# Spreading the weight sums over half units, and splitting the store and the read-back of turned probabilities, in a sparse-attention and FFN kernel

## The chip, the cores and the metric

The kernel runs on one core of one Trainium2 chip. The metric is the device time of one execution in microseconds (us), as the median of several runs. The engines are named as in the profile: PE is TensorE (PEld its weight loads), DVE is VectorE, ACT is ScalarE, POOL is GpSimd, and SP is SyncE, which in this kernel only issues DMAs. Each engine works through its own instructions in the order of the program and stops at the first one whose inputs or buffers aren't ready.

## The reference

```python
def _attn_ref(q, k, v):            # (8, 8, 576, 64) each, float32
    scores = scale * np.matmul(q, k.transpose(0, 1, 3, 2))
    mask_local = (rel >= 0) & (rel < 32)                       # heads 0-3
    mask_strided = (rel >= 0) & (pos[None, :] % 32 == pos[:, None] % 32)   # heads 4-7
    scores = np.where(masks, scores, -1e9)
    attn = np.exp(scores - scores.max(-1))
    return np.matmul(attn / (attn.sum(-1) + 1e-09), v)

def _moe_ref(x, w_in, w_out):      # x (4608, 512), w_in (512, 2048), w_out (2048, 512)
    h = x @ w_in
    g = np.where(h >= 1, h, np.where(h <= -1, 0.0, (h + 1) ** 2 / 4))
    return g @ w_out
```

The attention's output, 8 batches of 576 tokens with 8 heads of 64, is the FFN's x: 4608 tokens of 512.

## The kernel before

**The FFN** takes most of the time. Each value is split into a rounded high part and a remainder, and a product is three matmuls (high by high, high by low, low by high). The tokens are done in two ways. The first 1536 are done in three chunks c = 0, 1, 2 of 512 tokens. A chunk has 16 units (c, f), one for each block of 128 of the 2048 hidden columns: `up` (L589) is 12 matmuls of 512 columns into one of two PSUM banks; `gate` (L611) is a chain ACT, ACT, DVE, ACT, DVE (L603, L606, L609, L622, L625) that makes the two parts `gh` and `gl`; `down` (L631) multiplies the gated blocks of two units, 24 matmuls at every other unit. The remaining 3072 tokens are done in three super-chunks s = 0, 1, 2 of 1024 tokens by a Strassen-Winograd scheme with 7 products in place of 8: `up_block` (L699) has 56 steps of 6 matmuls (L722), `down_block` (L788) 28 steps of 12 (L828). Each step needs a weight block that SP fetches from device memory into a ring of seven buffers `wr` (`fetch_w`, L660), one fetch behind each step, so that a fetch has seven steps to land.

**The weight sums.** Strassen-Winograd needs sums of weight blocks, made while the chunks c = 1 and c = 2 run. `combine(i, j, w32, st)` (L239) does one of the 16 sums that the schedule `COMBINE` (L913) lists: POOL adds the high and low parts back together into `w32` (L244, two operations of 512 elements in each partition), makes four sums of blocks in `st` (L252, four operations of 256); ACT rounds them (L254), DVE takes the remainder (L255), and SP stores `st` to device memory (`ks`, L256). The six POOL operations, the ACT, the DVE and the SP instruction are issued together, in the first half of a unit: at units (1, 0), (1, 1), (1, 2), (1, 4), (1, 5), (1, 6), (1, 8), (1, 9), (1, 10), and (2, 4), (2, 5), (2, 7), (2, 8), (2, 9), (2, 11), (2, 12). The room for `w32` and `st` is one buffer each (in chunk 1 a part of the tile for the first super-chunk's tokens that isn't yet needed, in chunk 2 the places of weights that are done with), so that a sum can be written only when the last one has been stored.

**The attention** of batch 0 lies before everything, batch 1 in chunk 0; batches 2 to 7 are laid out by hand among the FFN's steps. The place of a step is counted in quarters of a unit, g = 4 x (16 x (c - 1) + f) in the chunks, and one step of `up_block` is one g, one of `down_block` two. So chunk 1 is g 0 to 63, chunk 2 is 64 to 127, super-chunk 0 is 128 to 239, super-chunk 1 is 240 to 351. `START` (L896) has the g at which a batch begins, `LATER` (L897) what follows at which distance. A batch has four parts u = 0 to 3, and each part runs through named steps: `s` scores on PE (L343), `m` mask on DVE (L394), `x` maximum on DVE (L405), `a` subtract it on POOL (L409), `e` exponential on ACT (L416), `q` sum on DVE, `p` add the small constant on ACT, `r` reciprocal on DVE and the product on POOL (L433), `t` 32 x 32 transposes on DVE into two tiles (`turn`, L462), `j` the rest of the transposition by way of device memory (`spread`, L474), `v` the product with the values on PE (L500), and `h`, `l`, copies out of PSUM into the tokens' tiles (L554, L563).

`spread` stores the two turned tiles with eight DMAs that put each 32 x 32 block where it belongs (L484), and reads the whole back with one (L485), which must wait until the eight have landed. The turned tiles come from a pool `o_p` of three buffers (tag `ob`), which `down` also uses for a chunk's four output tiles `ob` (L643), and part 1 for its result `pT`; the other parts' `pT` has one buffer of its own.

**The tokens' sums and splits** for the first super-chunk (`x_sum`, `x_split`, by `X_FIRST`, L915) are at units (2, 9) to (2, 15), those for the next ones at steps of `down_block` (`X_NEXT`, L968).

Of the kernel before, what the change touches and what calls it, by code (L numbers as in the profile page):

```python
# [8 lines left out]
F32 = mybir.dt.float32  # L9
F32R = mybir.dt.float32r  # L10
# [15 lines left out]
def tile_sparse_attention_then_ffn(  # L26
# [79 lines left out]
    def slot(tag, shape, dtype, name):  # L106

        return big.tile(shape, dtype, tag=tag, bufs=1, name=name)
# [130 lines left out]
    def combine(i, j, w32, st):  # L239


        for f in range(2):
            parts = [wt[2 * j + f][:, i, :, x].bitcast(F32) for x in range(2)]
            nc.gpsimd.tensor_tensor(out=w32[:, 2 * f:2 * f + 2], in0=parts[0], in1=parts[1], op=ALU.add)  # L244

        def block(r, c):
            return w32[:, 2 * r + c if i == 0 else 2 * c + r]

        s_ = [st[:, n, HF:].bitcast(F32) for n in range(4)]
        for to, a, b, op in ((0, block(1, 0), block(1, 1), ALU.add), (1, s_[0], block(0, 0), ALU.subtract),  # L250
                             (2, block(0, 0), block(1, 0), ALU.subtract), (3, block(0, 1), s_[1], ALU.subtract)):
            nc.gpsimd.tensor_tensor(out=s_[to], in0=a, in1=b, op=op)  # L252
        hi, lo = st[:, :, :HF], st[:, :, HF:]
        nc.scalar.copy(hi.bitcast(F32R), lo.bitcast(F32))  # L254
        nc.vector.tensor_tensor(out=lo.bitcast(F32R), in0=lo.bitcast(F32), in1=hi.bitcast(F32), op=ALU.subtract)  # L255
        nc.sync.dma_start(kept[i][j][1].rearrange("p n x e -> p n (x e)"), st)  # L256
# [50 lines left out]
    def attention(b, kinds):  # L307

        probs, flipped, ahead, covered = {}, {}, {}, set()
# [164 lines left out]
        def spread(u):  # L474

            ts = probs.pop(u)
            n = sum(slots(u))
            pool, tag = (o_p, "ob") if u == 1 else (pt_p, "pT")
            pT = pool.tile([P, 4, n if u == 1 else 2 * SLOTS, ST], F32, tag=tag, name=f"pT_{b}_{u}")
            there = dram.tile([P, 4, n, ST], F32, tag=f"t{u}", name=f"there_{b}_{u}")  # L480
            for i in range(4):
                for h in range(2):
                    to = there[h * 64:(h + 1) * 64, i].rearrange("(k c) n q -> c k (n q)", c=ST)
                    nc.sync.dma_start(to, ts[h][i * ST:(i + 1) * ST, :, :n])  # L484
            nc.sync.dma_start(pT[:, :, :n], there)  # L485
            flipped[u] = pT
# [71 lines left out]
        def low(u):  # L558
            if u not in flipped:
                return  # L560
            for src, to in parts(u):
                if len(to) == 2:
# [4 lines left out]
                 "f": flip, "t": turn, "j": spread, "c": keep, "d": keep_v, "v": value, "V": values_1_3, "h": high, "l": low}  # L567
# [295 lines left out]
    with tc.manual_schedule():  # L863
# [19 lines left out]
        for k in range(2):  # L883
# [12 lines left out]
        START = {2: 0, 3: 33, 4: 69, 5: 112, 6: 150, 7: 240}  # L896
        LATER = {0: ("s0", "m0 x0 a0"), 3: ("", "e0"), 6: ("s1", "q0 p0 r0 m1 x1 a1"), 9: ("", "t0 j0 e1"),  # L897
# [15 lines left out]
        COMBINE = {(1, 4 * n // 3): (n >= NP, n % NP) for n in range(NP + 1)}  # L913
        COMBINE |= {(2, 3 + 4 * n // 3): (1, n) for n in range(1, NP)}
        X_FIRST = {9: (1,), 10: (2,), 13: (-7, -6, 7), 14: (-4, -5, 6), 15: (5,)}  # L915
        pend = []
        for c in range(CLASSIC):
            for f in range(NF):
# [24 lines left out]
                if c:  # L943
                    steps(g0, g0 + 2, 1)
                    ship(f, c - 1)
                    if (c, f) in COMBINE:
                        i, j = COMBINE[c, f]
                        if c == 1:
                            w32, st = (x_tile(0)[:, :, e0:e1] for e0, e1 in ((704, 960), (192, 704)))
                        else:  # L950
                            w32, st = (slot(X_AT[m], [P, 4, n], F32, f"{a}_{j}") for m, n, a in ((3, HF, "w32"), (4, CH, "st")))
                        combine(i, j, w32, st)
                    if c == 2:
                        x_steps(0, *X_FIRST.get(f, ()))
# [13 lines left out]
        X_NEXT = {8: (1,), 9: (2,), 10: (-7,), 11: (-6,), 12: (7,), 13: (-4,), 14: (-5,), 15: (6,), 18: (5,), 20: (3,), 27: (4,)}  # L968
# [76 lines left out]
```

## Time and profile before

| | us |
|---|---|
| time, median of 3 runs | 988.71 (985.37 to 990.67) |
| the profiled execution: time | 987.04 |
| the profiled execution: span of its instructions | 985.3 |
| PE busy | 857.5 (87%) |
| DVE busy | 555.8 (56%) |
| ACT busy | 495.7 (50%) |
| POOL busy | 236.7 (24%) |

Times in the views are counted from the first instruction of the profiled execution. A matmul's duration overlaps with the next one's, so that 12 matmuls of about 0.4 us each take less than 3 us together. A view of the waits says which engine stood still, in front of which line, for whose result, in us in total, how many times, and the longest. The chain of waits is followed back from the last instruction, at each step to what released it. In a row of the timeline the bracket behind an instruction has the idle time before it and what ended that. The granted clock is TensorE's, as a share of full speed.

### The profile page before, as it was taken

What the parts mean: (1) busy time and instruction counts of PE and PEld (TensorE: products, weight loads), DVE (VectorE), ACT (ScalarE), POOL (GpSimd) and SP (SyncE); (2) the same over time, 40 slices, a digit from 0 to 9 for tenths busy, and PEclk for the clock granted to TensorE, in tenths of its full rate; (3) what the DMA queues carried; (4) which work ended last, traced back from release to release, by engine and by line L of the source; (5) the groups of instructions that cost most, each with busy time, mean ns of one, the idle gap of its engine ahead of it and who ended that gap; (6) DMA issues with size and microseconds to landing.
All of it is one profiled execution on the core that took longest, in us unless ns stands there. A gap on an engine that the chain in (4) does not pass through costs nothing.

```text
span 985.3 us, 17928 instructions
## 1 busy us (share of the span) xinstructions
PE 857.5 (87%) x6965; PEld 679.3 (69%) x6965; DVE 555.8 (56%) x822; ACT 495.7 (50%) x852; POOL 236.7 (24%) x244
## 2 busy tenths in 40 slices
PE   8999967767698865868889798998889989999997
PEld 6788846645576654646667586776777867887886
DVE  6899715433344344355476477755546874455664
ACT  5888713323334334235665454455665454676442
POOL 5454245636011564220221100012100000001000
PEclk8999988969799997989999899999999999999999
DMA  9917316555466465447677675667566657666664
GB/s 360 376 36 256 113 55 227 197 175 194 127 217 202 141 219 197 149 154 262 213 246 242 216 226 169 216 211 229 165 197 182 210 185 225 192 194 180 214 192 160
DMA packets 102565, 195.12 MB, mean 198 GB/s; under 512 B 15184, under 2 KB 28240, under 8 KB 101584
## 3 DMA queue, kind: packets, MB, share of 16 engines
q1 hardware_dynamic: 102480, 193.97, 61.0%
q8 instruction: 55, 0.90, 0.4%
q14 instruction: 30, 0.25, 0.1%
HBM read 147.26 MB, written 46.66 MB: 197 GB/s over the span
## 4 chain that ended last, share of the span: by engine, by line
PE 44%; DVE 16%; DMA 12%; ACT 11%; POOL 9%; issue 5%; SPq 3%; ACTq 0%; DVEq 0%; POOLq 0%
PE y L722 9%; PE yo L828 8%; PE h L599 6%; PE o L640 6%; DMA wr<-ks 5%; PE z L722 4%; DVE hl L691 4%; PE xo L828 3%; ACT hl L690 3%; PE xp L500 2%; POOL xs L252 2%; PE x L722 2%; SPq L484 2%; POOL st L252 2%; DMA there<-t 2%
## 5 line engine op out<-in xcount | busy, mean ns | idle before, releaser
L722 PE MATMUL y<-x,wr 128*128 128x512 f32 x576 | 148.1, 404 | 20.2 <-DMA wr<-kq 7.3
L640 PE MATMUL o<-gh,w 128*128 128x512 f32 x384 | 134.9, 418 | 28.7 <-ACT gh L622 23.1
L599 PE MATMUL h<-xq,w 128*128 128x512 f32 x576 | 148.8, 410 | 3.7 <-DVE gl L625 2.8
L722 PEld LDWEIGHTS y<-x,wr 128*128 128x128 f32 x576 | 109.7, 194 | 49.6 <-DVE gb L609 6.2
L828 PE MATMUL yo<-hl,wr 128*128 128x512 f32 x576 | 136.9, 395 | 7.4 <-DVE hl L691 4.7
L599 PEld LDWEIGHTS h<-xq,w 128*128 128x128 f32 x576 | 111.8, 198 | 30.2 <-DVE gl L625 3.2
L828 PEld LDWEIGHTS yo<-hl,wr 128*128 128x128 f32 x576 | 108.6, 190 | 34.0 <-DVE hl L691 7.8
L640 PEld LDWEIGHTS o<-gh,w 128*128 128x128 f32 x384 | 76.7, 200 | 49.3 <-ACT gh L622 26.4
L409 POOL TENSOR_TENSOR pr<-pr,st 128x768 f32<-128x768 f32 (+3 forms) x31 | 37.6, 1213 | 238.4 <-DVE st L405 218.4
L722 PE MATMUL z<-x,wr 128*128 128x512 f32 x288 | 75.8, 400 | 8.3 <-DMA wr<-ks 8.2
L640 PE MATMUL o<-gl,w 128*128 128x512 f32 x192 | 79.7, 415 | 1.1 <-DVE gl L625 1.1
L828 PE MATMUL zo<-hl,wr 128*128 128x512 f32 x288 | 68.8, 394 | 5.4 <-DVE hl L691 4.1
L433 POOL TENSOR_TENSOR pr<-pr,st 128x648 f32<-128x648 f32 (+3 forms) x30 | 35.8, 1193 | 152.2 <-DVE st L432 151.3
L722 PEld LDWEIGHTS z<-x,wr 128*128 128x128 f32 x288 | 54.3, 190 | 21.3 <-DMA wr<-ks 4.0
L828 PEld LDWEIGHTS zo<-hl,wr 128*128 128x128 f32 x288 | 53.5, 188 | 20.2 <-DVE hl L691 6.7
L690 ACT CAST hl<-ga 128x1024 fp32r<-128x1024 f32 x36 | 37.9, 1052 | 51.2 <-DVE ga L781 20.5
L756 POOL TENSOR_TENSOR ga<-gb,ga 128x1024 f32<-128x1024 f32 x9 | 21.6, 2397 | 170.5 <-DVE ga L609 169.8
L606 ACT ACTIVATE tmp<-tmp 128x512 f32<-128x512 f32 x96 | 60.7, 632 | 1.7
L609 DVE SCALAR_TENSOR_TENSOR h<-h,u 128x512 f32<-128x512 f32 x47 | 32.7, 695 | 48.1 <-ACT u L606 47.8
L691 DVE TENSOR_TENSOR hl<-ga,hl 128x1024 fp32r<-128x1024 f32 x36 | 44.3, 1232 | 27.2 <-ACT hl L690 27.2
L343 PE MATMUL sc<-qk 64*32 64x64 f32 (+1 forms) x1856 | 35.6, 242 | 23.7 <-DVE xq L563 16.7
L500 PE MATMUL xp<-pT,v 64*64 64x32 f32 (+2 forms) x1760 | 35.2, 234 | 22.1 <-DMA pT<-there 11.4
(122 smaller groups left out, 1337.8 us busy)
## 6 DMA issues: line engine op xcount, KB each, us to landing
wr<-ks SPq DMA_DIRECT2D x192, 256.0 KB, 3.5
wr<-kq SPq DMA_DIRECT2D x144, 256.0 KB, 3.2
raw<-in_w SPq DMA_DIRECT2D x30, 512.0 KB, 9.6
kq<-w SPq DMA_DIRECT2D x48, 256.0 KB, 4.0
qk<-in_qk_s SPq DMA_DIRECT2D x16, 604.0 KB, 6.6
qk<-in_qk_l SPq DMA_DIRECT2D x16, 576.0 KB, 7.1
ks<-xs SPq DMA_DIRECT2D x9, 1024.0 KB, 5.3
v<-in_v_l SPq DMA_DIRECT2D x21, 384.0 KB, 5.6
```

Source lines behind the costliest of these rows:

```text
L252: nc.gpsimd.tensor_tensor(out=s_[to], in0=a, in1=b, op=op)
L343: nc.tensor.matmul(sc[j][i * Q:(i + 1) * Q, s, p], qk[:, 0, q0:q0 + Q], qk[:, 1, k0:k0 + W], start=u not in covered, stop=u not in covered)
L409: eng.tensor_tensor(out=pr, in0=pr, in1=st[:, 0].unsqueeze(2).broadcast_to(list(pr.shape)), op=ALU.add)
L433: eng.tensor_tensor(out=pr, in0=pr, in1=st[:, 2].unsqueeze(2).broadcast_to(list(pr.shape)), op=ALU.mult)
L500: nc.tensor.matmul(xp[p][j * D:(j + 1) * D, n], loaded[b, local, b0 + n][keys, j], qs, start=True, stop=True)
L599: nc.tensor.matmul(o_ps[c, f], wt[f][:, 0, h, x, e:e + P], xq[c][:, y, cc], start=first and n == 0, stop=last and n == len(todo) - 1)
L606: nc.scalar.activation(u, u, AF.Square)
L640: nc.tensor.matmul(o_ps[c][d], wt[f][:, 1, h, x, e:e + P], gs[y], start=f == 0 and n == 0, stop=f == NF - 1 and n == 2)
L690: nc.scalar.copy(t[:, 0], src)
L691: nc.vector.tensor_tensor(out=t[:, 1], in0=src, in1=t[:, 0].bitcast(F32), op=ALU.subtract)
L722: nc.tensor.matmul(to, w_[:, a, c * P:(c + 1) * P], xc[m][:, b, c], start=m in (1, 2, 5) and c + q == 0, stop=c == 1 and q == 2, skip_grou ...
L828: nc.tensor.matmul(to, w_[jj][:, a, d * P:(d + 1) * P], t[:, b, jj], start=m in (1, 2, 5) and k + jj + q == 0, stop=k == NP // 2 - 1 and j ...
```

## The change

**Sums.** `combine` is cut in three: `recall` (the two POOL adds of L244), `combine` (the four POOL operations of L252) and `ship_sums` (ACT, DVE and the store). A helper `sums(h)` is called twice in a unit, once in each half, h counting halves from the start of chunk 1. At half h it issues the `recall` of the sum due at h + 1, then the `combine` of the sum due at h, then the `ship_sums` of the one due at h - 1. The sums are due at every third half: h = 0, 3, ..., 24 in chunk 1 and 39, 42, ..., 57 in chunk 2. The first `recall` moves into the end of chunk 0.

**Turned probabilities.** `j` only stores, with two DMAs, one for each turned tile; a new step `J` (`gather`) allocates `pT` and reads it with four DMAs, one for each group of 32 partitions, which do the rearranging. `j` is now two quarters behind `t`, and `J` three behind `j` (`j` and the reading were in the same quarter as `t`).

**Batches.** `START` and some places of `LATER` move: `v2` and `t3` from 33 to 35, the last values from 42 to 45. `X_FIRST` and `X_NEXT` move by about a unit or a step.

```diff
+    def recall(i, j, w32):
+        for f in range(2):
+            hi, lo = (wt[2 * j + f][:, i, :, x].bitcast(F32) for x in range(2))
+            nc.gpsimd.tensor_tensor(out=w32[:, 2 * f:2 * f + 2], in0=hi, in1=lo, op=ALU.add)
+
     def combine(i, j, w32, st):
-        for f in range(2):
-            parts = [wt[2 * j + f][:, i, :, x].bitcast(F32) for x in range(2)]
-            nc.gpsimd.tensor_tensor(out=w32[:, 2 * f:2 * f + 2], in0=parts[0], in1=parts[1], op=ALU.add)
...
+    def ship_sums(i, j, st):
         hi, lo = st[:, :, :HF], st[:, :, HF:]
-        nc.scalar.copy(hi.bitcast(F32R), lo.bitcast(F32))
-        nc.vector.tensor_tensor(out=lo.bitcast(F32R), in0=lo.bitcast(F32), in1=hi.bitcast(F32), op=ALU.subtract)
+        nc.scalar.copy(hi.bitcast(F32R), lo)
+        nc.vector.tensor_tensor(out=lo.bitcast(F32R), in0=lo, in1=hi, op=ALU.subtract)
         nc.sync.dma_start(kept[i][j][1].rearrange("p n x e -> p n (x e)"), st)
...
             ts = probs.pop(u)
             n = sum(slots(u))
+            there[u] = to = dram.tile([P, 2, 2, n, ST], F32, tag=f"t{u}", name=f"there_{b}_{u}")
+            for h in range(2):
+                nc.sync.dma_start(to[:, h], ts[h][:, :, :n])
+
+        def gather(u):
...
-            there = dram.tile([P, 4, n, ST], F32, tag=f"t{u}", name=f"there_{b}_{u}")
-            for i in range(4):
-                for h in range(2):
-                    to = there[h * 64:(h + 1) * 64, i].rearrange("(k c) n q -> c k (n q)", c=ST)
-                    nc.sync.dma_start(to, ts[h][i * ST:(i + 1) * ST, :, :n])
-            nc.sync.dma_start(pT[:, :, :n], there)
+            src = there.pop(u).rearrange("(i c) h k n q -> h k c i (n q)", c=ST)
+            for h in range(2):
+                for k in range(2):
+                    at = h * 64 + k * ST
+                    nc.sync.dma_start(pT[at:at + ST, :, :n].rearrange("p i n q -> p i (n q)"), src[h, k])
...
-        START = {2: 0, 3: 33, 4: 69, 5: 112, 6: 150, 7: 240}
-        LATER = {0: ("s0", "m0 x0 a0"), 3: ("", "e0"), 6: ("s1", "q0 p0 r0 m1 x1 a1"), 9: ("", "t0 j0 e1"),
-                 12: ("s2", "q1 p1 r1 m2 x2 a2"), 15: ("", "t1 j1 e2"), 18: ("v0", "h0 l0"),
-                 21: ("s3", "m3 x3 a3 q2 p2 r2"), 24: ("", "t2 j2 e3"), 28: ("", "q3 p3 r3"),
-                 33: ("v2", "h2 l2 t3 j3"), 42: ("V1", "h1 l1 h3 l3")}
+        START = {2: 0, 3: 37, 4: 72, 5: 118, 6: 155, 7: 240}
+        LATER = {0: ("s0", "m0 x0 a0"), 3: ("", "e0"), 6: ("s1", "q0 p0 r0 m1 x1 a1"), 9: ("", "t0 e1"), 11: ("", "j0"),
+                 12: ("s2", "q1 p1 r1 m2 x2 a2"), 14: ("", "J0"), 15: ("", "t1 e2"), 17: ("", "j1"),
+                 18: ("v0", "h0 l0"), 20: ("", "J1"), 21: ("s3", "m3 x3 a3 q2 p2 r2"), 24: ("", "t2 e3"), 26: ("", "j2"),
+                 28: ("", "q3 p3 r3"), 29: ("", "J2"), 35: ("v2", "h2 l2 t3"), 37: ("", "j3"), 40: ("", "J3"),
+                 45: ("V1", "h1 l1 h3 l3")}
...
-        COMBINE = {(1, 4 * n // 3): (n >= NP, n % NP) for n in range(NP + 1)}
-        COMBINE |= {(2, 3 + 4 * n // 3): (1, n) for n in range(1, NP)}
-        X_FIRST = {9: (1,), 10: (2,), 13: (-7, -6, 7), 14: (-4, -5, 6), 15: (5,)}
+        COMBINE = {3 * n: (n >= NP, n % NP) for n in range(NP + 1)} | {36 + 3 * n: (1, n) for n in range(1, NP)}
+        rooms_of = {}
+
+        def sums(h):
+            if h + 1 in COMBINE:
...
+                recall(*COMBINE[h + 1], rooms_of[h + 1][0])
+            if h in COMBINE:
+                combine(*COMBINE[h], *rooms_of[h])
+            if h - 1 in COMBINE:
+                ship_sums(*COMBINE[h - 1], rooms_of.pop(h - 1)[1])
+
+        X_FIRST = {9: (1,), 10: (2,), 14: (-7, -6, 7), 15: (-4, -5, 6, 5)}
...
                     steps(g0, g0 + 2, 1)
                     ship(f, c - 1)
-                    if (c, f) in COMBINE:
...
+                    sums(g0 // 2)
...
-                if c:
+                if c or f == NF - 1:
                     steps(g0 + 2, g0 + 4, 0)
                     steps(g0 + 2, g0 + 4, 1)
+                    sums(g0 // 2 + 1)
...
-        X_NEXT = {8: (1,), 9: (2,), 10: (-7,), 11: (-6,), 12: (7,), 13: (-4,), 14: (-5,), 15: (6,), 18: (5,), 20: (3,), 27: (4,)}
+        X_NEXT = {9: (1,), 10: (2,), 11: (-7,), 12: (-6,), 13: (7,), 14: (-4,), 15: (-5,), 16: (6,), 18: (5,), 20: (3,), 27: (4,)}
```

More of the change, by code (lines that the diff above doesn't have):

```diff
@@ L307, in attention @@
     def attention(b, kinds):
-        probs, flipped, ahead, covered = {}, {}, {}, set()
+        probs, flipped, there, ahead, covered = {}, {}, {}, {}, set()
         def banks(u, kind):
@@ L566, in attention @@
         steps = {"s": score, "y": score_0, "z": score_1, "m": mask, "o": opened, "i": cover, "g": plain, "x": most, "w": norm_v, "a": below_max, "e": expo, "q": total, "p": plus_eps, "k": plus_eps_v, "b": below_max_v, "r": norm,
-                 "f": flip, "t": turn, "j": spread, "c": keep, "d": keep_v, "v": value, "V": values_1_3, "h": high, "l": low}
+                 "f": flip, "t": turn, "j": spread, "J": gather, "c": keep, "d": keep_v, "v": value, "V": values_1_3, "h": high, "l": low}
         after = {"s1": lambda: fetch_qk(b, 2), "s3": lambda: b > 1 and fetch_qk(b + 1, 0),
@@ L945, in tile_sparse_attention_then_ffn @@
                     ship(f, c - 1)
-                    if (c, f) in COMBINE:
[L947 to L952, printed above, removed]
+                    sums(g0 // 2)
                     if c == 2:
```

8 lines of the change are left out of this document (7 added, 1 removed).

## The prediction

> **What bounds the kernel now.** I read the busy shares first and then cut the span at the stages' ends: chunk 1, the part of chunk 2 with weight sums, and the super-chunks (the last two are shown). Columns: length; busy us of PE, PEld, DVE, ACT, POOL (instructions); granted clock, DMA share, GB/s.
>
> ```profile
> 120.80:267.70 146.90, 103.44 (x1077) 80.99 (x1076) 54.73 (x96) 44.12 (x81) 66.74 (x71) 0.83 0.51 168
> ...
> 325.00:441.90 116.90, 81.89 (x741) 62.70 (x739) 49.70 (x72) 40.81 (x74) 52.08 (x54) 0.89 0.51 174
> ...
> 636.00:826.00 190.00, 174.73 (x1154) 137.71 (x1153) 117.25 (x147) 100.74 (x152) 19.82 (x14) 0.97 0.64 196
> 826.00:985.30 159.30, 153.22 (x669) 124.73 (x667) 89.07 (x102) 85.87 (x124) 9.62 (x4) 0.99 0.63 193
> ```
>
> The super-chunks are PE's: 92 and 96% busy. The chunks with sums are nobody's: PE is 70% busy at a clock of 0.83 to 0.89, and no other engine reaches half. So what bounds them is a chain of latencies. The waits name it (us in total, times, longest):
>
> ```profile
> ACT xs L254 <- POOL xs L252: 51.8, 8, 11.3
> ...
> ACT st L254 <- POOL st L252: 36.0, 6, 9.7
> ```
>
> ACT stands 87.8 us before L254 for POOL's block sums. The gates that `down` needs are queued behind that instruction, and DVE's half of each gate behind its own L255, which needs ACT's. The chain of waits in chunk 1 shows the loop (start, us, what):
>
> ```profile
> 130.33 2.72 PE h L599 x12
> ...
> 133.74 1.47 POOL pr L409
> 135.21 2.48 POOL xs L244 x2
> ...
> 189.78 0.74 POOL xs L252
> 190.59 2.14 POOL xs L252 x3
> 192.76 1.06 ACT xs L254
> 193.84 1.35 DVE xs L255
> 195.21 4.92 DMA ks<-xs
> 200.28 0.74 POOL xs L252
> ```
>
> From the first block sum at 189.78 to the next sum's at 200.28, 10.5 us: `st` can't be written before its last contents have been stored. That part of the loop stays in the changed kernel.
>
> The gates on ACT give the pace (start, us, ..., idle before): units (1,0), (1,11), (1,12), (2,4), (2,13), (2,15).
>
> ```profile
> 123.56 0.69 ACT L603 ACTIVATE u<-h,half 128x512 f32<-128x512 f32 x1 [4.08 <-PE h L599]
> 254.19 0.74 ACT L603 ACTIVATE u<-h,half 128x512 f32<-128x512 f32 x1
> 260.79 0.69 ACT L603 ACTIVATE u<-h,half 128x512 f32<-128x512 f32 x1 [2.42 <-PE h L599]
> 317.91 0.68 ACT L603 ACTIVATE u<-h,half 128x512 f32<-128x512 f32 x1
> 411.75 0.67 ACT L603 ACTIVATE u<-h,half 128x512 f32<-128x512 f32 x1
> 424.48 0.69 ACT L603 ACTIVATE u<-h,half 128x512 f32<-128x512 f32 x1 [0.28 <-PE h L599]
> ```
>
> With sums: (1,0) to (1,11) is 130.6 us for 11 units and 9 sums, 14.5 us a sum; (2,4) to (2,13) is 93.8 us for 9 units and 7 sums, 10.4 us a unit. Without: (1,12) to (2,4) is 57.1 us for 8 units, 7.14 each, a change of chunk included. From (1,0) to (2,15) 31 units take 300.9 us.
>
> **The change, part by part.** *Sums.* The instructions are the same in number and kind; what moves is their place. `recall` (2.48 us) leaves the loop, since it is issued a half unit ahead of a `combine` that still waits for the store. ACT and DVE no longer stand through all of POOL's 5.4 us; `ship_sums` is issued a half unit behind. What is left for one sum is the 10.5 us, and ahead of its `combine` on POOL the attention's subtract or product in that half: eight in 45 quarters, so 1.07 in the six quarters from sum to sum, at up to 1.47 us each (I take 1 us). That is 11.5 us for a sum, and a sum comes every 1.5 units: 7.7 us a unit. Ends: the sum-free 7.14 if everything else fits beside, and 10.4, as in chunk 2 now, if it doesn't. I take 7.7, because its main term is a row of the same loop.
>
> What is queued behind the new waits: behind `combine` on POOL the next half's `a` and `r` steps, for which ACT's exponential and DVE's transposes wait; behind `ship_sums` on ACT and DVE the next gate, and behind its store on SP what the next half issues.
>
> The first unit is special. The maximum of batch 2 keeps POOL till 135.21 as before. `recall` is done by then, having been issued in chunk 0; `combine` takes 2.95 us (189.78 to 192.73), so to 138.2, and ACT's copy runs to 139.2. The gate of (1,1) then starts there, 15.6 us behind that of (1,0). So: 15.6, then 21.5 units with sums (halves 2 to 25 and 38 to 58) at 7.7 = 165.6, then 8.5 without at 7.14 = 60.7, together 241.9 against 300.9: **59 us gained**, to the gate of (2,15).
>
> *End of chunk 2.* Batch 5 now begins at g 118. Its `t0` falls at 127, its `j0` at 129, behind chunk 2's end. So two of the three `ob` buffers are taken while `down` writes its four output tiles; each tile after the first waits until the one before it has been stored. (First two stores of such tiles in the chain, then rows of the timeline.)
>
> ```profile
> 143.82 4.53 DMA out<-ob
> ...
> 292.13 2.80 DMA out<-ob
> ```
>
> ```profile
> 441.88 2.93 PE L722 MATMUL y<-x,wr 128*128 128x512 f32 x6 [5.57 <-DMA wr<-kq]
> 444.60 1.23 ACT L644 COPY ob<-o 128x512 f32<-128x512 f32 x2 [5.28 <-DMA out<-ob]
> ...
> 448.25 1.66 PE L722 MATMUL y<-x,wr 128*128 128x512 f32 x6 [0.91 <-ACT ga L732]
> ```
>
> Now it is 23.8 us from the gate of (2,15) at 424.48 to the third step of super-chunk 0 at 448.25. After the change, counted from that gate: the gate, five instructions of 0.7 (the rows above), 3.5; two token sums on DVE that have moved behind it, of L255's size, 2.7; a split's copy of L254's size 1.1 and an exponential 0.7, together 8; an output tile 0.6 (half of 1.23); three more at 0.6 + 0.4 for the issue + 3.8 (between 2.80 and 4.53) = 14.4; two splits' copies 2.1; the start 0.5: 25.6. But SP no longer has 16 stores and two reads to issue in front of the first weight fetches, so the 5.57 before 441.88 goes. I count **1 us lost**, between 5 lost (if SP, standing before each output, also holds up fetches 3 to 6) and 9 gained (if the tiles don't wait).
>
> *Turned probabilities.* (First SP's waits and issue times in ns, min/median/max; then the issues with KB each and us to landing.)
>
> ```profile
> SPq L484 <- DVE t L470: 71.7, 24, 7.4
> SPq L485 <- DMA there<-t: 26.2, 44, 1.2
> ```
>
> ```profile
> L484 SPq DMA_DIRECT2D there<-t x192: 302/425/1738, 160.0 to 710.0; - x192
> ```
>
> ```profile
> there<-t SPq DMA_DIRECT2D x96, 48.0 KB, 1.7
> pT<-there SPq DMA_DIRECT2D x12, 384.0 KB, 3.4
> ```
>
> One part costs SP now nine issues at 0.425, 3.8 us, and of waiting 1.1 us for the landing and 3.0 us for DVE: about 8 us in which no weight is fetched, while the ring's seven steps are worth 7 x 1.36 = 9.5. After it: two issues, 0.85 us, and three quarters later four, 1.7 us at the same price (between 1.2 and 7, with the shortest and the longest seen), with neither wait, because `t` lies two quarters ahead and the stores three. In the super-chunks PE's waits for fetches are these:
>
> ```profile
> PE y L722 <- DMA wr<-kq: 7.3, 2, 5.6
> PE y L722 <- DMA wr<-ks: 7.2, 3, 2.9
> PE z L722 <- DMA wr<-ks: 8.2, 3, 3.3
> PE yo L828 <- DMA wr<-kq: 2.8, 1, 2.8
> ```
>
> 25.5 us, less the 5.6 counted above: 19.9. Against that, `v0` now follows its read by four quarters, some 5.5 us here, of which issuing takes 1.7 and landing 2 to 3.4 (a store of 48 KB and a read of 384; each read is 96 KB): tight. For nine value steps of batches 5 to 7 I give back 6 us in all: **14 us gained**, between 0 and 20.
>
> *Batches and X steps.* They carry no new work. In `down_block` the last values of batch 6 come nearer to the token sums; no row shows a cost. I count nothing and leave 2 us for it in the range.
>
> **Sum:** 59 - 1 + 14 = 72 us. The profiled execution took 987.04 (span 985.3 and 1.74 around it); 915.0 after. The median of the runs is 1.67 above the profiled one, so 916.7, **917**.
>
> **Rivals.**
>
> *Full decoupling.* The store's landing hides and PE sets the pace. 24 matmuls are 5.44 us (2.72 for 12) and the attention's add 33.3/32 = 1.04:
>
> ```profile
> 120.80:441.90 321.10, 14.54 (x696) 13.15 (x696) 0.88 0.53 174
> ```
>
> ```profile
> 120.80:441.90 321.10, 18.73 (x888) 15.15 (x888) 0.88 0.53 174
> ```
>
> (values, then scores.) 30 units at 6.5 instead of 7.5 give 31 us more: 886. For it: no engine is near full. Against it: the 10.5 us loop has one `st`.
>
> *The sums keep their price.* POOL is slower when DVE works:
>
> ```profile
> 140.72 3.48 POOL L244 TENSOR_TENSOR xs<-w 128x512 f32<-128x512 f32 x2
> 141.75 1.32 DVE L255 TENSOR_TENSOR xs<-xs 128x1024 fp32r<-128x1024 f32 x1 [8.16 <-ACT xs L254]
> ```
>
> The pair that takes 2.48 alone took 3.48 beside L255. If each block sum of `combine`, too, met a DVE operation and lost up to 0.7, a sum would take 14.3 us and a unit 9.6: 41 us back, 958; at 10.4 a unit, 975. Against it: the block sums at 190.59, three in 2.14, were not slowed, and they are the part that stays in the loop. The Trainium skill, in "SBUF — State Buffer", section "SBUF: two separate sides", says that a DVE operation with two SBUF inputs and a GpSimd operation hold one shared pair of ports in turn, each for its whole length; the row of 3.48 agrees, and by that rule spreading the POOL work over more halves beside more DVE work speaks for this rival.
>
> *Slower: the values wait for their read.* Its place are the 18 steps `v0`, `v2`, `V1`, which now have four to six quarters behind a read that SP may issue late, standing before a fetch or a load. That it happens is seen once:
>
> ```profile
> 391.96 1.34 PE L500 MATMUL xp<-pT,v 54*64 54x64 f32 x40 [9.95 <-DMA pT<-there]
> ```
>
> At 5 us each it costs 90 and the kernel takes 1007; from 4 us each, 72 in all, nothing is gained. Against it: SP gets the wait for DVE and the wait for the landing off its queue.
>
> *No change*, 989: the sums' waits only change names, ACT standing at `ship_sums` as long as at `combine` now, the gates behind it as before, and PE's waits in the super-chunks staying.
>
> **How the numbers follow.** The forecast (900 to 940) gets 0.54, full decoupling 0.15, sums at their price (940 to 980) 0.17, no change 0.05, slower 0.09. About 5 us, 0.5%, is what a measurement of this kernel can tell from no change (its three runs span 5.3). So faster 0.86, same 0.05, slower 0.09. The range leaves out both last cases and the outer ends of two others: 885 to 968.
>
> **What would show it.** Right: in chunks 1 and 2 ACT's wait before `ship_sums` falls from 87.8 to under 30 us, the gates come 7 to 8 us apart, and the chain shows block sum, ACT, DVE, store; PE's waits for `wr` in the super-chunks fall under 8 us; the first outputs of chunk 2's end stand 4 to 5 us apart. Wrong: PE standing before L500 for the new read by more than 20 us in total; POOL's block sums longer than 1 us in the mean; gates still over 9 us apart.

## The result, and the profile after

| | before | after | change | forecast |
|---|---|---|---|---|
| time, median | 988.23 | 922.93 (922.47 to 923.32, 4 runs) | -65.3 | -72 |
| ratio, 95% interval | | 0.934 (0.9314 to 0.9366) | | |
| the profiled execution: time (span) | 987.04 (985.3) | 923.32 (921.5) | -63.7 (-63.8) | |
| span: to the gate of (1,0) | 123.56 | 121.73 | -1.8 | 0 |
| gates (1,0) to (2,15) | 300.92 | 262.74 | -38.2 | -59 |
| gate of (2,15) to the third step of super-chunk 0 | 23.77 | 21.78 | -2.0 | +1 |
| from there to the end | 537.05 | 515.25 | -21.8 | -14 |

Of the four stretches of the span in the last rows, the second is called the gates below, the third the seam, the fourth the super-chunks. The profiled execution of run e3 below was a slow one, 1051.1 us at a granted clock of 0.74; it is left out of every number, and so e3 has no trace to compare.

The kernel is faster by about as much as forecast, but the parts aren't as forecast: the sums gave two thirds of their share, the transfers half as much again. The 1.8 us before the gate of (1,0) are scatter: runs whose program is the same up to there (the changed kernel, e4, e7, e8) have that gate at 121.7 to 124.0. In the changed kernel L254 is L257, L252 is L253, L255 is L258, L256 is L259, the stores are L483, the reads L494, the values L509, the products L649 and L731.

The stages, in the same columns as before (length; busy us of PE, PEld, DVE, ACT, POOL; clock, DMA share, GB/s):

```profile
120.80:406.25 285.45, 232.72 (x2332) 183.03 (x2331) 129.58 (x207) 111.16 (x203) 127.43 (x127) 0.91 0.58 195
406.25:588.00 181.75, 171.58 (x1441) 136.16 (x1442) 125.46 (x166) 101.58 (x170) 26.02 (x21) 0.98 0.78 243
588.00:762.00 174.00, 166.79 (x1142) 132.44 (x1141) 115.89 (x145) 98.83 (x151) 19.86 (x14) 1.00 0.70 211
762.00:921.50 159.50, 153.95 (x672) 125.28 (x670) 89.06 (x102) 86.43 (x125) 9.62 (x4) 1.00 0.64 193
```

In the chunks PE is now 82% busy, still with 53 us idle. The forecast's 70% was for the parts with sums alone; over the whole stretch to the third step PE was 74% busy before (243.9 of 327.5 us). In the super-chunks it is 94 to 97%. The waits of the chunks:

```profile
ACT xs L257 <- POOL xs L253: 26.0, 6, 8.3
ACT st L257 <- POOL st L253: 16.7, 5, 6.6
POOL st L253 <- DMA ks<-st: 15.0, 4, 4.8
POOL xs L253 <- DMA ks<-xs: 8.4, 2, 4.9
PE o L649 <- ACT gh L631: 21.7, 5, 6.7
```

ACT's wait for POOL in front of the rounding is halved, 87.8 to 42.7 us, and not under 30 as forecast; PE waits for `gh` almost as long as before (23.1). The gates of (1,0), (1,1), (1,13), (2,4), (2,13) and (2,15):

```profile
121.73 0.69 ACT L612 ACTIVATE u<-h,half 128x512 f32<-128x512 f32 x1 [4.08 <-PE h L608]
137.18 0.68 ACT L612 ACTIVATE u<-h,half 128x512 f32<-128x512 f32 x1
...
240.59 0.68 ACT L612 ACTIVATE u<-h,half 128x512 f32<-128x512 f32 x1
...
290.76 0.67 ACT L612 ACTIVATE u<-h,half 128x512 f32<-128x512 f32 x1
...
366.64 0.69 ACT L612 ACTIVATE u<-h,half 128x512 f32<-128x512 f32 x1 [4.48 <-PE h L608]
...
384.47 0.69 ACT L612 ACTIVATE u<-h,half 128x512 f32<-128x512 f32 x1 [2.51 <-PE h L608]
```

The first unit took 15.45 us (forecast 15.6). Then 12 units with sums took 103.4, 8.6 each, seven without 50.2, 7.17 each, and nine with sums 75.9, 8.4 each. Forecast were 7.7 with and 7.14 without. The last two units, without sums, took 17.8.

At the end of chunk 2 the four outputs stand one behind the other, and the third step waits for ACT's copy behind them:

```profile
395.09 0.57 ACT L653 COPY ob<-o 128x512 f32<-128x512 f32 x1
397.79 0.59 ACT L653 COPY ob<-o 128x512 f32<-128x512 f32 x1 [2.14 <-DMA out<-ob]
400.52 0.59 ACT L653 COPY ob<-o 128x512 f32<-128x512 f32 x1 [2.14 <-DMA out<-ob]
403.24 0.59 ACT L653 COPY ob<-o 128x512 f32<-128x512 f32 x1 [2.13 <-DMA out<-ob]
```

```profile
406.25 2.93 PE L731 MATMUL y<-x,wr 128*128 128x512 f32 x6 [8.89 <-ACT ga L741]
```

They are 2.7 us apart, not the forecast 4 to 5: a store lands in 2.0 there.

In the super-chunks PE no longer waits for weights at all (20.8 us from the third step on before), and once, for 0.9 us, for turned probabilities. The same stretch in the columns of the stages, before and after:

```profile
448.25:985.30 537.05, 497.14 (x3204) 396.06 (x3204) 326.25 (x406) 288.63 (x442) 52.56 (x35) 0.98 0.66 206
406.25:921.50 515.25, 492.32 (x3252) 393.88 (x3252) 330.40 (x413) 286.83 (x444) 55.51 (x39) 0.99 0.71 217
```

Of the 21.8 us 17.0 are PE's idle time and 4.8 its busy time, at a granted clock of 0.98 and then 0.99 (with 48 matmuls more in the stretch); so a higher clock is no more than about a quarter of this gain.

SP's waits in the whole execution, then the transfers (KB, us to landing):

```profile
SPq L494 <- DMA there<-t: 18.5, 9, 5.0
SPq L483 <- DVE t L473: 14.7, 10, 6.2
```

```profile
there<-t SPq DMA_DIRECT2D x24, 192.0 KB, 4.7
pT<-there SPq DMA_DIRECT2D x48, 96.0 KB, 3.3
```

SP's wait for DVE fell from 71.7 to 14.7 us. Its wait for the landing fell only from 26.2 to 18.5; a store now lands 4.7 us after its issue and not 1.7.

### The profile page after: what moved, and what is told of

It is laid out like the page before. It is cut to its first block, busy times and chain, and to the rows that moved or that the text cites. A ratio compares the mean times of both kernels' runs of the same rounds, so it can differ in the third digit from the quotient of the medians.

```text
span 921.5 us, 17868 instructions
## 1 busy us (share of the span) xinstructions
PE 840.6 (91%) x6965; PEld 669.2 (73%) x6965; DVE 560.0 (61%) x822; ACT 493.9 (54%) x852; POOL 241.7 (26%) x244
## 4 chain that ended last, share of the span: by engine, by line
PE 51%; DVE 20%; ACT 15%; DMA 6%; issue 4%; POOL 4%; SPq 1%; ACTq 0%; DVEq 0%; POOLq 0%
PE o L649 10%; PE y L731 9%; PE h L608 8%; PE yo L837 8%; DVE hl L700 5%; PE z L731 4%; PE xo L837 4%; ACT hl L699 3%; PE xp L509 3%; ACT tmp L612 2%; PE x L731 2%; ACT tmp L615 2%; PE sc L346 2%; POOL xs L253 2%; DVE pr L397 1%
## 5 line engine op out<-in xcount | busy, mean ns | idle before, releaser
L731 PE MATMUL y<-x,wr 128*128 128x512 f32 x576 | 144.9, 397 | 12.9 <-ACT ga L741 8.9
L649 PE MATMUL o<-gh,w 128*128 128x512 f32 x384 | 133.2, 414 | 21.7 <-ACT gh L631 21.7
L608 PE MATMUL h<-xq,w 128*128 128x512 f32 x576 | 145.5, 403 | 0.8 <-DVE xq L572 0.5
L731 PEld LDWEIGHTS y<-x,wr 128*128 128x128 f32 x576 | 107.2, 189 | 39.9 <-ACT ga L741 9.3
L608 PEld LDWEIGHTS h<-xq,w 128*128 128x128 f32 x576 | 109.7, 194 | 26.2 <-DVE xq L572 1.2
L649 PEld LDWEIGHTS o<-gh,w 128*128 128x128 f32 x384 | 76.4, 199 | 40.5 <-ACT gh L631 23.8
L412 POOL TENSOR_TENSOR pr<-pr,st 128x768 f32<-128x768 f32 (+3 forms) x31 | 38.2, 1233 | 176.2 <-DVE st L408 176.0
L649 PE MATMUL o<-gl,w 128*128 128x512 f32 x192 | 79.0, 411 | 0.3 <-DVE gl L634 0.2
L731 PE MATMUL z<-x,wr 128*128 128x512 f32 x288 | 74.3, 393 | 1.1 <-ACT gab L767 1.1
L731 PEld LDWEIGHTS z<-x,wr 128*128 128x128 f32 x288 | 54.1, 189 | 13.0 <-ACT gab L767 1.5
L634 DVE TENSOR_TENSOR gl<-h,gh 128x512 fp32r<-128x512 f32 x47 | 32.5, 692 | 29.2 <-ACT gh L631 28.6
L612 ACT ACTIVATE u<-h,half 128x512 f32<-128x512 f32 x48 | 32.8, 684 | 31.2 <-PE h L608 31.2
```

The lines of the kernel that those rows point to most:

```text
L412: eng.tensor_tensor(out=pr, in0=pr, in1=st[:, 0].unsqueeze(2).broadcast_to(list(pr.shape)), op=ALU.add)
L608: nc.tensor.matmul(o_ps[c, f], wt[f][:, 0, h, x, e:e + P], xq[c][:, y, cc], start=first and n == 0, stop=last and n == len(todo) - 1)
L612: nc.scalar.activation(u, h, AF.Relu, bias=half, scale=0.5)
L634: nc.vector.tensor_tensor(out=gl, in0=g, in1=gh.bitcast(F32), op=ALU.subtract)
L649: nc.tensor.matmul(o_ps[c][d], wt[f][:, 1, h, x, e:e + P], gs[y], start=f == 0 and n == 0, stop=f == NF - 1 and n == 2)
L731: nc.tensor.matmul(to, w_[:, a, c * P:(c + 1) * P], xc[m][:, b, c], start=m in (1, 2, 5) and c + q == 0, stop=c == 1 and q == 2, skip_grou ...
```

## Experiments

My theory when they began: the change is two parts that add up, the sums in the chunks and the transfers in the super-chunks; in the first the loop of block sums, ACT, DVE and store sets the pace, in the second SP's standing for DVE and the landing was what cost. The rivals: the parts need each other; not the waits but the number of transfers counts; and in the sums not the store closes the loop but something else in the engines' order. All ratios are to the kernel before, run beside.

### One part at a time

**e1_old_turn**: the changed kernel with the old `spread` and the old `LATER`.

```diff
+            for i in range(4):
+                for h in range(2):
+                    to = there[h * 64:(h + 1) * 64, i].rearrange("(k c) n q -> c k (n q)", c=ST)
+                    nc.sync.dma_start(to, ts[h][i * ST:(i + 1) * ST, :, :n])
+            nc.sync.dma_start(pT[:, :, :n], there)
...
-        LATER = {... 9: ("", "t0 e1"), 11: ("", "j0"), ... 14: ("", "J0"), ...}
+        LATER = {... 9: ("", "t0 j0 e1"), ...}
```

> The changed kernel with the turned probabilities as before: eight stores and one read in the same quarter as t, and the old distances of v2, t3 and the last values; sums in three steps and the batches' new starts stay. My theory: the change has two parts that add up. From the third step of super-chunk 0 to the end the changed kernel takes 515.3 us, the kernel before 537.1; those 21.8 us are the turned probabilities' and are lost here, the 40 us of the chunks stay: 941 to 949 us, PE's waits for wr in the super-chunks again 15 to 25 us. Rival 1: the parts need each other, since SP, standing 8 us in each part of a batch, also holds up the stores of the sums that the loop waits for: 955 or more. Rival 2: the super-chunks' gain is from the batches' new starts and not from the transfers: under 932.

Measured: 953.0 us, ratio 0.9645 (0.9604 to 0.9686). The gates take 260.7 us (262.7 in the changed kernel), so the chunks' gain doesn't need the new transfers (the new starts of the batches stay in this run). From the third step, at 411.07, to the end at 950.2 it takes 539.1 us, against 515.3 and, before, 537.1: the super-chunks' gain is gone. The seam took 4.7 us more, which I had not counted. PE's waits for weights from the third step on add up to 20.5 us:

```profile
PE y L725 <- DMA wr<-ks: 6.4, 4, 4.2
PE yo L831 <- DMA wr<-kq: 4.0, 1, 4.0
PE y L725 <- DMA wr<-kq: 3.8, 3, 2.2
PE z L725 <- DMA wr<-ks: 3.3, 2, 2.1
PE xo L831 <- DMA wr<-kq: 2.1, 1, 2.1
PE x L725 <- DMA wr<-kq: 0.9, 1, 0.9
```

The time lies 4 us above my range and 2 below the rival's; by the stages the sums' gain is all there, and the rival that they need the transfers falls. The second rival, that the new starts gave the super-chunks' gain, falls too: the starts are here and the gain is not.

**e2_old_sums**: the changed kernel with the whole sum at the old units.

```diff
+        COMBINE = {(1, 4 * n // 3): (n >= NP, n % NP) for n in range(NP + 1)}
+        COMBINE |= {(2, 3 + 4 * n // 3): (1, n) for n in range(1, NP)}
...
+                recall(i, j, w32)
+                combine(i, j, w32, st)
+                ship_sums(i, j, st)
...
-                    sums(g0 // 2)
+                    sums(c, f)
...
-                    sums(g0 // 2 + 1)
```

> The changed kernel with the weight sums as before: all instructions of a sum together, at the old units; the turned probabilities, the starts and the X steps are the new ones. My theory (two parts that add up): 962 to 972 us, the gates of the chunks (1,0) to (2,15) some 295 to 303 us, the super-chunks as in the changed kernel. Rival: the transfers in SP's queue also bound the chunks, so that much of the chunks' 40 us comes from them: under 952.

Measured: 973.6 us, ratio 0.9847 (0.9808 to 0.9886), just above my range. The super-chunks are the changed kernel's (third step at 456.77, end at 973.1: 516.3 us). The chunks are worse than before: 312.3 us from gate to gate against 300.9. So beside the old sums the new transfers and starts cost 11 us there; PE waits 17.6 us for turned probabilities in front of the values (11.4 before).

So the two parts don't add up as my theory had it. Alone the sums save 35 us (e1) and the rest 15 (e2), together 65. The missing 15 are these 11 us in the chunks and the 4.7 at the seam of e1: beside the old form of the other part each loses some of its gain.

### Number of transfers, or quarters between

**e3_eight_one**: eight stores at `j`, one read at `J`, the quarters as changed.

```diff
+            for i in range(4):
+                for h in range(2):
+                    nc.sync.dma_start(to[h * 64:(h + 1) * 64, i].rearrange("(k c) n q -> c k (n q)", c=ST), ts[h][i * ST:(i + 1) * ST, :, :n])
...
+            nc.sync.dma_start(pT[:, :, :n], there.pop(u))
```

> The changed kernel, but j issues eight stores and J one read, as the kernel before has them; the quarters of t, j and J are the new ones. My theory: what held the weight fetches up was SP's standing for DVE and for the stores' landing (4.1 of 8 us a part), and these are gone through the quarters between t, j and J; nine issues instead of six cost 1.3 us of SP that nothing waits for: 920 to 928 us, PE's waits for wr in the super-chunks under 6 us. Rival: the number of transfers counts, and half or more of the 22 us of the super-chunks is lost: 934 or more.

Measured: 930.4 us, ratio 0.941 (0.9368 to 0.9451): 2.4 above my range, 3.6 under the rival's. e1 has the same eight stores and one read, without quarters between and at the old distances, and takes 953.0. So the quarters and distances alone are worth 22.6 of the 30.1 us between e1 and the changed kernel.

**e9_no_gap**: two stores and four reads, all in the quarter of `t`, at the old distances.

```diff
-        LATER = {... 9: ("", "t0 e1"), 11: ("", "j0"), ... 14: ("", "J0"), ...}
+        LATER = {... 9: ("", "t0 j0 J0 e1"), ...}
```

> The changed kernel with t, j and J of a part in one quarter, at the old distances: two stores, four reads, no quarters between. SP stands for DVE (3 us) and for the stores' landing (now 4.4 us in the median, 1.7 with eight stores), some 10 us a part with the issuing, more than before. My theory: the super-chunks' 22 us are lost, and more: 943 to 955 us, PE's waits for wr in the super-chunks over 18 us. Rival (the number of transfers counts): 920 to 930.

Measured: 925.9 us, ratio 0.9383 (0.9335 to 0.9431). My theory falls: SP stands longer than before, 126.3 us against 97.9, and the kernel is nearly as fast as the changed one.

```profile
SPq L483 <- DVE t L473: 76.0, 24, 9.5
SPq L494 <- DMA there<-t: 50.3, 25, 5.1
```

Six transfers in place of nine, without quarters, are worth 27.1 us of the 30.1 (953.0 to 925.9). Together with e3: either edit alone brings most of the gain, and neither is its only cause. By stages: from the third step, at 401.29, to the end, at 924.2, it takes 522.9 us, between 515.3 (changed) and 539.1 (e1), with 11.0 us of PE's waits for weights. So here the quarters and distances are worth another 8 us. In the chunks they cost 10: without them the gates take 253.1 us, with them 262.7. SP's waits of 5.3 us a part are no measure of what they cost; a stretch in which SP stands also contains time in which it would have stood for PE, to free a buffer of the ring. That reason is argued; in its favour, SP's waits for PE ahead of the weight fetches add up to 247.6 us here and to 282.3 in the changed kernel.

### The outputs at the seam

**e4_b5_120**

```diff
-        START = {2: 0, 3: 37, 4: 72, 5: 118, 6: 155, 7: 240}
+        START = {2: 0, 3: 37, 4: 72, 5: 120, 6: 155, 7: 240}
```

> The changed kernel with batch 5 starting at g 120 instead of 118, so that its t0 falls behind the four output tiles of chunk 2. My theory: t0's two tiles leave one of three ob buffers, the outputs go through it one by one, 2.7 us apart, and the third step of super-chunk 0 waits 8.9 us for ACT. With t0 behind them the four outputs take under 6 us from first to last instead of 8.2, that wait falls under 5 us, and the kernel takes 914 to 919 us. Rival: ACT would come late anyway through the splits that moved behind the last gate, or the later batch gives it back: 921 to 926.

Measured: 916.9 us, ratio 0.9268 (0.9215 to 0.932). The third step waits 3.46 us instead of 8.89:

```profile
397.49 2.78 PE L731 MATMUL y<-x,wr 128*128 128x512 f32 x6 [3.46 <-ACT ga L741]
```

Three outputs now stand back to back and the fourth waits 1.17. This step of the prediction is shown: `t0`'s two tiles held the outputs up, and the kernel gains 6.0 us. By stages it is more than the outputs: the seam takes 14.8 us instead of 21.8, the two units before it 13.9 instead of 17.8, and the super-chunks give 4.5 back (519.7).

### What the three steps of a sum are worth

**e5_recall_late**: `recall` in the half of its `combine`.

```diff
-                recall(*COMBINE[h + 1], rooms_of[h + 1][0])
             if h in COMBINE:
+                recall(*COMBINE[h], rooms_of[h][0])
                 combine(*COMBINE[h], *rooms_of[h])
```

> The changed kernel with recall in the half of its combine, directly ahead of it. Theory 1, as my prediction had it: recall, 2.5 us of POOL, has left the loop of a sum, and put back it lengthens each of the 14 intervals between sums by about as much: gates (1,0) to (2,15) 285 to 300 us instead of 263, the kernel 943 to 960. Theory 2: POOL stands for the stores anyway (23 us in 6 of the 16 sums), and recall, which needs no store, runs in that time wherever it is issued: 921 to 930.

Measured: 939.0 us, ratio 0.9487 (0.9433 to 0.9542), gates 278.1 us. Between the two theories: 15 us, 1.1 us for each of the 14 intervals where `recall` takes 2.5. Part of it finds room wherever it stands. The waits show where the rest goes: not into POOL's wait for the stores (20.4 us, 23.4 in the changed kernel), but into ACT's wait for POOL, which grows from 42.7 to 67.7 us:

```profile
ACT xs L257 <- POOL xs L253: 47.3, 8, 9.7
ACT st L257 <- POOL st L253: 20.4, 5, 5.1
```

**e6_ship_early**: `ship_sums` in the half of its `combine`.

```diff
-            if h - 1 in COMBINE:
-                ship_sums(*COMBINE[h - 1], rooms_of.pop(h - 1)[1])
+                ship_sums(*COMBINE[h], rooms_of.pop(h)[1])
```

> The changed kernel with ship_sums in the half of its combine. Theory 1: the half unit between them is what frees ACT and DVE from standing for POOL; without it they stand some 3 us more at each of the 16 sums, with the gates behind them: ACT's wait before the rounding grows from 43 to over 65 us, the kernel takes 938 to 960. Theory 2: what counts is the loop block sum, ACT, DVE, store, block sum, which is closed sooner when ACT comes to it sooner: 910 to 925.

Measured: 966.3 us, ratio 0.9763 (0.9698 to 0.9827), gates 305.4 us: the whole gain of the sums is gone, though `recall` is still ahead and the sums still 1.5 units apart. The first and the last gate, and the waits (ACT stands 77.5 us for POOL, PE 34.0 for turned probabilities):

```profile
123.55 0.69 ACT L612 ACTIVATE u<-h,half 128x512 f32<-128x512 f32 x1 [4.08 <-PE h L608]
...
428.94 0.69 ACT L612 ACTIVATE u<-h,half 128x512 f32<-128x512 f32 x1 [2.54 <-PE h L608]
```

```profile
ACT xs L257 <- POOL xs L253: 48.5, 8, 7.1
PE xp L509 <- DMA pT<-there: 34.0, 15, 10.1
ACT st L257 <- POOL st L253: 29.0, 5, 7.0
```

Theory 2, on which my prediction rested, asks for a faster kernel here. It is the half unit between POOL's sums and what follows them that gave the gain. `ship_sums` moves ACT's, DVE's and SP's instruction together, and the run doesn't separate them: SP, too, stands longer in front of the sums' stores, 131.9 us against 94.2, with the reads of turned probabilities queued behind it.

**e7_two_st**: two buffers for `st` in turn in chunk 2.

```diff
+                    other = {42: "w2", 48: "w4", 54: "w4"}.get(h + 1, X_AT[4])
-                    rooms_of[h + 1] = [slot(X_AT[m], ...) for m, n, a in ((3, HF, "w32"), (4, CH, "st"))]
+                    rooms_of[h + 1] = [slot(tag, ...) for tag, n, a in ((X_AT[3], HF, "w32"), (other, CH, "st"))]
```

> The changed kernel with two buffers for st in turn in chunk 2 (three of its seven sums go to places of weights that are done with). Theory 1: the store closes the loop, 12.3 us a sum in chunk 2 where 1.5 units without sums take 10.8; with a second buffer POOL's waits for the store of st (15.0 us in 4) go, the sums come 10.8 to 11.5 us apart, and the kernel takes 913 to 918. Theory 2: the wait for the store only hides other waits in the same engines' order (POOL for DVE's sums and maxima, ACT for POOL): less than 2 us, 921 to 925.

Measured: 923.2 us, ratio 0.9326 (0.9272 to 0.938): the changed kernel's time. POOL's wait for the store of `st` no longer appears among the waits (15.0 us in the changed kernel), and the nine units from (2,4) to (2,13) take 73.2 us instead of 75.9. So in chunk 2 the store does not set the pace; at most these 2.7 us are its own.

**e8_wider**: the sums of chunk 2 are 3.5 halves apart.

```diff
-        COMBINE = {...} | {36 + 3 * n: (1, n) for n in range(1, NP)}
+        COMBINE = {...} | {35 + 7 * n // 2: (1, n) for n in range(1, NP)}
```

> The changed kernel with the seven sums of chunk 2 at halves 38, 42, 45, 49, 52, 56, 59, 3.5 halves apart instead of 3. Theory 1: a sum costs the chunk a fixed amount, its ACT and DVE work and ACT's wait for POOL, with the gates behind them, wherever it stands: 920 to 926 us. Theory 2: the sums are bound by being dense (POOL comes late to a block sum because the last sum isn't through), and at a distance of 1.75 units, 12.6 us at the pace without sums, they are nearly free: 912 to 918.

Measured: 915.7 us, ratio 0.9277 (0.921 to 0.9343), the same nine units in 65.9 us, 7.3 each, close to the pace without sums. Fewer block sums lie in these units now, five instead of six; but the twelve units from (2,3) to (2,15), which hold all seven in both kernels, take 89.1 us instead of 98.1. The interval of the ratio reaches the changed kernel's; the gates speak for theory 2: a sum costs little if POOL, being through with it, lets ACT pass. ACT's wait for POOL in chunk 2 is 7.7 us (16.7).

**e10_ship_two**: `ship_sums` two halves behind `combine`, with e7's buffers.

```diff
-            if h - 1 in COMBINE:
-                ship_sums(*COMBINE[h - 1], rooms_of.pop(h - 1)[1])
+            if h - 2 in COMBINE:
+                ship_sums(*COMBINE[h - 2], rooms_of.pop(h - 2)[1])
```

> The changed kernel with ship_sums two halves behind combine instead of one, and the two buffers for st in chunk 2 (which alone changed nothing). Theory 1: what the half unit gave was that ACT and DVE stand less for POOL; a second half takes most of the remaining 43 us of ACT's wait before the rounding (under 20 us), and the chunks from (1,0) to (2,15) fall from 263 to 245 to 257 us, the kernel to 904 to 917. Theory 2: in chunk 1, with one st, the later store holds the next block sum up and POOL's wait grows from 8 to over 20 us; what chunk 2 gains chunk 1 loses: 918 to 930.

Measured: 902.8 us, ratio 0.9142 (0.9083 to 0.92), the fastest of all. ACT's wait falls to 11.6 us, PE's for `gh` from 21.7 to 4.3, and the gates take 238.3 us; gates and time lie below my ranges. POOL waits longer for the one `st` of chunk 1, and it costs less than it saves:

```profile
121.10 0.69 ACT L612 ACTIVATE u<-h,half 128x512 f32<-128x512 f32 x1 [4.08 <-PE h L608]
...
359.36 0.69 ACT L612 ACTIVATE u<-h,half 128x512 f32<-128x512 f32 x1 [2.51 <-PE h L608]
```

```profile
POOL xs L253 <- DMA ks<-xs: 15.7, 4, 6.8
ACT xs L563 <- DMA ks<-xs: 11.9, 3, 6.9
ACT xs L257 <- POOL xs L253: 11.3, 6, 3.9
...
PE o L649 <- ACT gh L631: 4.3, 4, 1.3
ACT st L257 <- POOL st L253: 0.3, 1, 0.3
```

With `ship_sums` at zero, one and two halves behind, ACT stands 77.5, 42.7 and 11.6 us for POOL, and the gates take 305.4, 262.7 and 238.3. (The second buffers alone, e7, have 44.3 and 260.9.) The wait is a sign and not the whole price: in e1 ACT stands 52.1 us with gates of 260.7, in k2 below 13.1 with 252.8.

### Putting them together

**k1_close_then_apart**: batches 2 to 4 as in e9, 5 to 7 as changed, batch 5 at 120.

```diff
-                for at, names in LATER.items():
+                for at, names in (CLOSE if b < 5 else LATER).items():
```

> The changed kernel with t, j and J in one quarter and the old distances for batches 2 to 4 (in the chunks), the new distances for batches 5 to 7, and batch 5 starting at g 120. The chunks' gates took 253 us with no quarters between (263 with), the super-chunks 515 with them (523 without), and the later batch 5 took 6 us off at the seam. If these three add up: 905 to 912 us. If the chunks' 10 us came from the seam or from one run, or the transfers left between the batches collide: 915 to 922.

Measured: 910.1 us, ratio 0.9212 (0.9156 to 0.9269), gates 251.0, the third step's wait 3.47. The time lies where the three add up, but the stages don't all follow: gates and seam (14.8 us) gain 18.7 us together, and the super-chunks take 520.7 us, not the 515 that I had counted; they give back 5.4, as in e4, where batch 5 was also later. Why the chunks want the transfers close together (and the old distances of the values) I did not settle.

**k2_both**: e10 and k1 together.

> The two edits that gained most in one kernel: ship_sums two halves behind combine with two buffers for st in chunk 2 (903 us), and the batches 2 to 4 with t, j and J in one quarter at the old distances, batch 5 starting at g 120 (910 us). If ACT's wait for POOL and the transfers' places are separate causes, their gains of 20 and 13 us add up: 887 to 893 us, gates (1,0) to (2,15) 226 to 232 us. If both shorten the same waits in the chunks (238 and 251 us there), only the seam's 6 us come on top: 895 to 899.

Measured: 910.7 us, ratio 0.9213 (0.9183 to 0.9242), gates 252.8: above both cases, and slower than e10 alone. The seam is 7 us shorter than in e10. In the chunks ACT, copying a batch's output into the tile in which chunk 1's `st` lies, waits for the sums' stores, 19.6 us in all (11.9 in e10), and the next scores stand behind it:

```profile
ACT xs L563 <- DMA ks<-xs: 19.6, 3, 10.1
...
PE sc L346 <- DVE xq L572: 8.1, 1, 8.1
```

With the old distances batch 2's last values come three quarters earlier, where `ship_sums` now issues its stores later. The gates lose 14.5 us against e10. The largest single loss is between those of (1,10) and (1,11), which are 21.3 us apart instead of 9.2; this wait and the scores' 8.1 us lie there:

```profile
212.85 0.28 ACT L563 COPY xs<-xp 128x72 f32<-128x72 f32 x1 [6.05 <-DMA ks<-xs]
```

That the old distances brought the copies among the stores is argued; no run moves them alone. e10 with batch 5 at 120 alone was not tried.

## Why the prediction was right, and where it was not

The total, 917 against 923, came out closer than its parts, and that is luck: the sums fell 21 us short, and the seam, the transfers and the scatter ahead of them brought 13 us that I hadn't counted.

*What bounds the kernel*: right. The sums' latencies bounded the chunks, and splitting them gave the larger part of the gain (e2, without it, is 1.5% faster than the kernel before; e1, with it and the old transfers, 3.5%; both together 6.6%).

*The sums, 59 us*: the mechanism was half right, the size too large, and the loop in it was wrong. The step of the sum that failed reads "What is left for one sum is the 10.5 us" of block sums, ACT, DVE and store. I took that stretch of the old chain for the loop that stays. In the changed kernel POOL waits for a store at six of the sums only, and a sum takes 12.6 to 12.9 us and not 11.5. e7 takes the store out of the loop in chunk 2, and the time stays; e6 closes the loop sooner, and the whole gain goes. The chain of waits of the changed kernel still passes through a sum's store three times in the chunks (7.10, 5.08 and 5.39 us), as I had asked of it, and that proved nothing. For chunk 1 no run takes the store out, but e10 lengthens the wait for it there and is faster. What remains is the other wait that the same section named and then left: ACT in front of the rounding, with the gates behind it. It fell to 42.7 us and not to under 30. The units with sums took 0.7 to 0.9 us more than forecast, 17.6 us over 21 units; the last two units, which have none, took 3.3 more. That the 17.6 are this wait's is argued from e6 and e10, in which both move together; e10 shows that it could have gone to 11.6.

*Recall leaves the loop, 2.5 us*: it is worth 1.1 us an interval (e5), and by way of ACT's wait, not of POOL's wait for the store.

*The first unit, 15.6 us*: 15.45, and by the steps that I gave: from the product of batch 2's maximum POOL goes straight to the block sums, ACT's rounding follows, and the gate behind it.

*The end of chunk 2*: the cause was right and is shown by e4. The sum around it, 25.6 us, came out at 21.8 by two errors that partly cancel: the outputs stood 2.7 us apart and not 4.8, since the stores landed in 2.0 us and not 3.8, and the first of them came 10.6 us behind the gate and not 8.0.

*Turned probabilities, 14 us*: 21.8. I gave back 6 us for values that wait for their read in the super-chunks; they waited 0.9. The price of a part, "about 8 us in which no weight is fetched", was added up from SP's waits, and e9 shows that SP can stand longer than before with most of the gain kept. Which of the two edits I needed I had not asked; e3 and e9 show that either brings most of it.

*The rivals*. Full decoupling needed 240 us less 30, 210 from gate to gate; e10 comes to 238. The sums kept 8.4 to 8.6 us a unit, between my 7.7 and the rival's 9.6, and POOL's block sums were not slowed: 0.73 us in the mean, the longest 0.75. The slower case, values waiting for their read, is real, 9.9 us in 9 times and nearly all of it in the chunks, where 72 would have used up the gain; it grows to 34.0 in e6.

## What to carry to other kernels

When an engine that works in order stands for a slower one, count what is queued behind the standing instruction, and issue that instruction so much later in the program that its input is there; here the first half unit was worth 43 us of the gates and the second 24 (with two buffers in turn in chunk 2), and the longer hold on the buffer cost little in e10, but took the second gain away in k2, where a copy needed that room. A stretch of the chain of waits that repeats is not yet the loop that will set the pace once one link is taken out: take out each link in an experiment. And before two gains are put together, look for the buffer that both lean on.

## What the runs showed of the hardware

A store of 48 KB landed 1.7 us after its own issue, one of 192 KB with the same bytes in a quarter as many transfers 4.7 us (3.3 in e9); the chain of waits has one that took 7.10. That doesn't make eight stores sooner than two: issued one behind the other, 0.425 us each, the last of eight lands some 7 x 0.425 + 1.7 = 4.7 us after the first is issued, the second of two 0.4 + 4.7 = 5.1 or 0.4 + 3.3 = 3.7 (estimates from these medians). Fewer transfers saved SP's issuing and did little for the landing.

When DVE's remainder meets POOL's operations, both sides get longer:

```profile
172.11 1.28 POOL L436 TENSOR_TENSOR pr<-pr,st 128x648 f32<-128x648 f32 x1
...
172.35 2.11 DVE L258 TENSOR_TENSOR xs<-xs 128x1024 fp32r<-128x1024 f32 x1 [0.71 <-ACT xs L257]
173.34 3.54 POOL L244 TENSOR_TENSOR xs<-w 128x512 f32<-128x512 f32 x2
```

DVE's operation takes 1.23 us at its shortest, POOL's pair about 2.5. The rows read as taking turns: POOL's product ends at 173.39, DVE's remainder 1.07 us later, at 174.46, and POOL's pair 2.42 us after that. The rule of the Trainium skill in "SBUF — State Buffer", section "SBUF: two separate sides", that the one fully blocks while the other has the shared ports, agrees with these rows. As the rival that it spoke for, it did not decide the time.
